# Two of four row tiles turned by DMA instead of PE, and the last weights moved behind those transposes

## The chip, the cores and the metric

The kernel runs on one core of a Trainium2 chip. The metric is device time in microseconds (us); lower is better. All timed runs of this study were in the fast state; the few that ran at a lower mean granted clock (0.991; the granted clock is the share of its full speed at which the matmul engine may run) are named where they matter.

One core has a matmul engine (PE, whose weight loads are listed as PEld), VectorE (DVE), ScalarE (ACT), GpSimd (POOL) and a queue of DMA issues on SyncE (SPq). ACT can issue DMAs too (ACTq). The profile counts the core's DMA work over 16 DMA engines. In its views `arena` is the kernel's one large buffer on the chip and PS are the banks that PE writes. A DMA has *landed* when all its parts have arrived; the *slack* of a transfer is the time from its landing to its first use.

## The reference, cut to what matters

```python
x = A_x                                   # 2048 rows of 512, bf16
xn = layernorm(x)                         # (x - mean) / sqrt(var + eps)
return x + ssm(xn) + (gelu(xn @ w_gate) * (xn @ w_up)) @ w_down   # 1376 hidden columns
# ssm: a complex diagonal recurrence over the rows, between two projections, plus xn * Dskip
```

The rows are worked in four blocks of 512, and a block in four tiles of 128 rows. This kernel's matmuls take a tile with its 512 features on the partitions (the rows of the buffer), so each normalised tile has to be turned.

## The kernel before

A helper records every operation with what it reads and writes; a scheduler orders DVE, ACT and POOL, while PE and the sync queue keep the order of the program. Block 0 is special: PE would otherwise wait for the normalisation, so its four tiles are only centred, turned on PE, and matmuls on the gate and up columns 0 to 895 start at once. The division by sigma is done afterwards, as the `scale` of the gelu and of the product. The rest of the hidden columns (896 to 1375, weight chunk 3) and the Bu projections use the normalised block turned by DMA, with 512 rows per matmul; I call those matmuls *block-wide*.

```python
def cent_T(j, banks, engs="A"):           # turn centred tile j on PE: 4 transposes + copy from PSUM by ACT
    ...
    ins_ = e.transpose(pt[:, 128*q:128*(q+1)], XN[j].ap[:, 128*k:128*(k+1)], IDN.ap)
    ...
FR = ((0, 192), (192, 384), (384, 640), (640, 896))
def unit(j, r):                           # tile j, column range r: gate and up matmuls, gelu, product
    bank = next_bank()
    GT_mm(j, r, bank, [0, 1])             # lhs XCd(j, k): the tile turned on PE
    GT_evac(j, r, bank, rss[j])           # rss[j] = 1/sigma of tile j
# loads on the sync queue, in this order (x tile 1, second half of gate chunk 0 and the
# three parameter rows are on the scalar queue):
#   x0, gate0 (first half), x2, up0, x3, gate1, up1, gate2, up2, gate3, up3,
#   transpose of the parameters, transposes of tiles 0, 1, 2, 3, x of block 1, B ...
fill(2); cent_T(0, tb, "AA"); cent_T(1, [wb])
... # tile 0 and 1, ranges 0 and 1: gate columns, then up columns; cent_T(2) in between
unit(2, 0); unit(2, 1)
cent_T(3, [ub[0, 0]])
unit(0, 2); unit(1, 2); unit(3, 0); unit(3, 1); unit(2, 2); unit(3, 2)
norms(0, [2, 3], mn2, rq2, 2)
TR(0)                                     # all four tiles turned by DMA into XNT[0]
ld_x(1)
for j in range(4): unit(j, 3)
...
GU(0, [7, 8, 9, 10])                      # block-wide, weight chunk 3
BU(0)                                     # block-wide Bu projections
```

Of the kernel before, what the change touches and what calls it, by code (L numbers as in the profile page):

```python
# [77 lines left out]
class Sched:  # L78
# [95 lines left out]
    def _backward(self, span):  # L174
# [11 lines left out]
        while n:  # L186
            best = None
            for e in ENGINES:
                if e in INORDER:
                    if not last[e] or left[last[e][-1].id]:  # L190
                        continue
                    op = last[e][-1]
                else:
                    if not ready[e]:
                        continue
                    op = max(ready[e], key=lambda o: (min(busy[e], late[o.id]), o.finish, o.id))
                end = late[op.id] if op.kind == "dma" else min(busy[e], late[op.id])
                if best is None or end > best[0]:
                    best = (end, op)
            end, op = best  # L200
            e = op.eng
            if e in INORDER:
                last[e].pop()
            else:
                ready[e].remove(op)
            begin[op.id] = end - op.dur
            if op.kind == "dma":
                begin[op.id] = min(begin[op.id], busy[e] - op.issue)
                busy[e] = begin[op.id]
            else:  # L210
                busy[e] = begin[op.id]
            n -= 1
            for d in op.deps:
                late[d.id] = min(late[d.id], begin[op.id] - LAT(d, op))
                left[d.id] -= 1
                if left[d.id] == 0 and d.eng not in INORDER:
                    ready[d.eng].append(d)
        return begin

    def _forward(self, prio):  # L220
# [13 lines left out]
        def rdy_time(op):  # L234
            return max([d.finish + LAT(d, op) for d in op.deps] + [op.nb])
# [55 lines left out]
    def emit(self):  # L291
# [19 lines left out]
        for e in ENGINES:  # L311
            seen = {}
            prog = []
            for op in order[e]:
                need = {}
                for d in op.deps:
                    if d.kind == "eng" and d.eng == e and (e == "tensor" or d is op.behind):
                        continue
# [43 lines left out]
def d_pe(n_list):  # L362
    return sum(n / 2.4 + 2.5 for n in n_list)
# [3 lines left out]
def d_dve_ts4x(n): return 220.0 + 0.26 * n  # L367
# [5 lines left out]
def build(nc, ins, out):  # L373
    with ExitStack() as es:
# [135 lines left out]
        ld_w(WU, WUc, ins["B_w_up"], 0)  # L510
        ld_x0(3)
        for ci in (1, 2):
            ld_w(WG, WGc, ins["B_w_gate"], ci)
            ld_w(WU, WUc, ins["B_w_up"], ci)

        def load_par():
            for q, nm in enumerate(("A_log_dt", "A_Lambda_re", "A_Lambda_im")):
                S.dma(lambda e, q=q, nm=nm: e.dma_start(PROW.ap[4 * q:4 * q + 4, :], ins[nm].rearrange("(s p) -> s p", p=128)),
                      1024, writes=[PROWq[q]], tag="ld_" + nm, queue="scalar", after=[half])

        def tr_par():
            S.dma(lambda e: e.dma_start_transpose(PAR.ap.rearrange("p q t -> p (q t)").unsqueeze(1), PROW16.ap), 4096,
                  reads=PROWq, writes=[PAR], tag="tr_par", issue=900.0)
# [11 lines left out]

        def load_W():
            ld_w(WG, WGc, ins["B_w_gate"], 3)
            ld_w(WU, WUc, ins["B_w_up"], 3)
# [147 lines left out]
        def GT_mm(j, r, bank, us, ks=range(KD)):  # L686
# [8 lines left out]
            def f(e):  # L695
                ins_ = None
                for k in ks:
                    ins_ = e.matmul(dst, XCd(j, k), WGU[:, us[0]:us[-1] + 1, k, f0:f1], start=(k == 0), stop=(k == KD - 1))  # L698
                return ins_
            PE(f, d_pe([w * len(us)] * len(ks)), Wc + XCs[j][ks[0] // 2:ks[-1] // 2 + 1], [BANK[bank]], "GT")  # L700

        def GT_evac(j, r, bank, rs):
            f0, f1 = FR[r]
            w = f1 - f0
            GATE["nh"] = kk = (GATE["nh"] + 1) % 3
            sc, rb = rs
            GATE["last_gelu"] = ACT(lambda e: e.activation(GG[kk].ap[:, 0:w], PS[bank][:, 0:w], ACTF.Gelu_apprx_tanh, scale=sc),  # L707
                                    d_act(w, 1), [BANK[bank], rb], [GG[kk]], "gelu")
            hp = Buf("H0_%d_%d" % (j, r), "sb", H0[j].lo + 2 * f0, H0[j].lo + 2 * f1)
# [9 lines left out]
        def TR(b):  # L719
            tts = list(range(4 * b, 4 * b + 4))  # L720
            for j, tt in enumerate(tts):
# [213 lines left out]
        load_par()  # L935
        load_W()
        tr_par()
# [3 lines left out]
        ch(V(lambda e: e.tensor_scalar(XN[1].ap, X[1].ap, NM1.ap, None, ALU.add), d_dve_ts4x(512), [X[1], NM1], [XN[1]], "sub"))  # L941
        ch(*stats(0, 1))
        op, mn0, qb0, rq0 = root(0, 0, 2)
        ch(op)
        ch(*stats(0, 2)); ch(sub(2))
        ch(recip(qb0, rq0))
# [3 lines left out]
        cent_T(1, [wb])  # L950
        ub = {(j, r): next_bank() for j in range(2) for r in range(2)}
# [5 lines left out]
        for j in range(2):  # L957
            ch(norms(0, [j], mn0, rq0, 0))
        ch(*stats(0, 3)); ch(sub(3))
        op, mn2, qb2, rq2 = root(0, 2, 4)  # L960
        ch(op)
        ch(recip(qb2, rq2))
        rss = [(rq.ap[:, i:i + 1], rq) for rq in (rq0, rq2) for i in range(2)]
# [6 lines left out]
        for j in range(2):  # L970
            for r in range(2):
                GT_mm(j, r, ub[j, r], [1])
                GT_evac(j, r, ub[j, r], rss[j])
                if j == 0 and r == 0:
                    cent_T(2, tb)
        unit(2, 0); unit(2, 1)
        cent_T(3, [ub[0, 0]])
        unit(0, 2)
        unit(1, 2)
        unit(3, 0); unit(3, 1)  # L980
        unit(2, 2); unit(3, 2)
        norms(0, [2, 3], mn2, rq2, 2)
        TR(0)
        ld_x(1)
        for j in range(4):
            unit(j, 3)
# [89 lines left out]
```

## Time and profile before

| what | before | how to read it |
|---|---|---|
| time, median (all runs beside the change) | 178.34 us (177.96 to 178.51, 6 runs) | device time |
| span of the profiled run | 176.6 us | one execution |
| PE busy | 98% of the span | part 1 of the page |
| chain of waits on PE | 1.02 to 174.1 us without a gap over 0.05 us | the view of the chain |
| last up chunk landed | 13.1 us (issued 7.21, 5.9 us to landing) | the view of DMA issues |

The chain of waits, cut to its first 25 us, for the kernel before. Columns: start in us, length in us, engine or cause, output and line, number of instructions. L698 is the matmuls of single tiles, L673 the PE transposes, L823 the block-wide gate and up matmuls, L734 the Bu matmuls.

```profile
...
7.51 0.22 PE PS L673 x4
7.73 2.32 PE PS L698 x20
10.05 0.22 PE PS L673 x4
10.27 8.21 PE PS L698 x40
...
18.53 5.13 PE PS L823 x23
...
24.98 2.16 PE PS L734 x10
```

PE works through. The two lines of L673 at 7.51 and 10.05 are what the change takes away, 0.22 us each.

The waits of PE in the whole run, for the kernel before: the engine and line that waited, for whom, total us, times, longest.

```profile
PE PS L914 <- DVE arena L479: 1.0, 1, 1.0
```

Only the wait for the first operand at the start.

The sync queue's issues, in order of time, for the kernel before (start, length of the issue, line, operation).

```profile
5.94 1.23 SPq L494 DMA_DIRECT2D arena<-in_B_w_gate_dram  x1
7.21 0.69 SPq L494 DMA_DIRECT2D arena<-in_B_w_up_dram  x1
8.03 1.29 SPq L522 DMA_TRANSPOSE arena<-arena  x1
9.37 5.18 SPq L722 DMA_TRANSPOSE arena<-arena  x4
```

Both last weight chunks are issued right behind the others. They land at 11.8 and 13.1 us; the four transposes, issued from 9.4 to 14.5 us, land between 13.8 and 15.8. PE needs the tiles and the gate chunk at about 18.3 us and the up chunk at about 19.2.

### The profile page before, as it was taken

The numbers are of one execution on the slowest core, as the hardware profiler recorded it, in microseconds if no ns is written. First come the engines' busy times: TensorE is split into PE (matmuls) and PEld (weight loads), VectorE is DVE, ScalarE is ACT, GpSimd is POOL, SyncE is SP. The second block draws the span as 40 slices with busy tenths as digits, with TensorE's granted clock in tenths as the row PEclk, the third lists the DMA queues.
The fourth block names the chain that finished last, engine by engine and source line by source line (L and its number), as shares of the span: only waits on it lengthen the run. The fifth ranks groups of instructions, "written<-read, shape, count | busy, mean of one in ns | idle before, by whom it ended". The sixth has DMA issues, their size and how long they took to land.

```text
span 176.6 us, 2492 instructions
## 1 busy us (share of the span) xinstructions
PE 172.3 (98%) x873; PEld 84.5 (48%) x888; DVE 160.7 (91%) x283; ACT 89.5 (51%) x169; POOL 11.4 (6%) x25
## 2 busy tenths in 40 slices
PE   7999999999999999999999999999999999999994
PEld 2954464444544444444644444444454444444453
DVE  6979999998999979799999999899999999999811
ACT  5565678999666997003676692000767780000000
POOL 3212240200000000500000000000000000000000
PEclk9999999999999999999999999999999999999999
DMA  6997999676899000011025000100001000000311
GB/s 173 312 322 181 162 231 127 63 146 121 176 248 303 11 0 0 0 61 59 4 44 105 2 0 0 33 30 30 30 0 30 4 0 0 0 0 30 111 60 43
DMA packets 33396, 14.36 MB, mean 81 GB/s; under 512 B 23688, under 2 KB 33384, under 8 KB 33384
## 3 DMA queue, kind: packets, MB, share of 16 engines
q1 hardware_dynamic: 32944, 13.87, 35.0%
q10 hardware_dynamic: 440, 0.33, 0.6%
q8 instruction: 7, 0.11, 0.3%
q14 instruction: 5, 0.04, 0.1%
HBM read 6.46 MB, written 2.10 MB: 48 GB/s over the span
## 4 chain that ended last, share of the span: by engine, by line
PE 98%; issue 1%; DVE 0%
PE PS L864 37%; PE PS L823 32%; PE PS L734 16%; PE PS L698 7%; PE PS L797 3%; PE PS L914 2%; PE PS L673 1%; PE PS L921 0%; DVE arena L882 0%; DVE arena L479 0%; DVE arena L478 0%
## 5 line engine op out<-in xcount | busy, mean ns | idle before, releaser
L864 PE MATMUL PS<-arena 128*128 128x512 bf16 (+3 forms) x317 | 65.9, 366 | 0.3
L823 PE MATMUL PS<-arena 128*128 128x512 bf16 x258 | 57.5, 379 | 0.3
L864 PEld LDWEIGHTS PS<-arena 128*128 128x128 bf16 (+1 forms) x323 | 30.9, 98 | 35.2
L823 PEld LDWEIGHTS PS<-arena 128*128 128x128 bf16 x264 | 25.8, 98 | 30.4
L838 ACT ACTIVATE arena<-PS 128x512 bf16<-128x512 f32 x33 | 19.8, 601 | 37.5 <-PE PS L823 33.7
L767 DVE TENSOR_TENSOR_SCAN arena<-arena 128x512 bf16<-128x512 f32 x32 | 38.7, 1255 | 0.0
L734 PE MATMUL PS<-arena 128*128 128x512 bf16 x125 | 27.8, 379 | 0.2
L842 ACT ACTIVATE arena<-PS 128x512 bf16<-128x512 f32 x33 | 19.8, 598 | 5.1 <-PE PS L823 4.9
L734 PEld LDWEIGHTS PS<-arena 128*128 128x128 bf16 x128 | 12.5, 98 | 14.9
L856 ACT ACTIVATE PS<-arena 128x512 f32<-128x512 bf16 (+2 forms) x17 | 9.3, 581 | 17.5 <-DVE arena L882 17.1
L738 ACT ACTIVATE arena<-PS 128x512 bf16<-128x512 f32 x32 | 17.3, 602 | 1.3 <-PE PS L734 1.3
L882 DVE TENSOR_TENSOR arena<-PS,arena 128x512 bf16<-128x512 f32 (+2 forms) x17 | 10.8, 654 | 6.7 <-PE PS L864 6.6
L844 DVE TENSOR_TENSOR arena<-arena 128x512 bf16<-128x512 bf16 x33 | 13.2, 416 | 1.1 <-ACT arena L842 1.1
L698 PE MATMUL PS<-arena 128*128 128x192 bf16 (+2 forms) x80 | 13.0, 320 | 0.0
L624 DVE BATCH_NORM_STATS2 arena<-arena 128x6 f32<-128x512 bf16 x16 | 10.3, 686 | 0.6 <-DMA arena<-in_A_x_dram 0.6
L698 PEld LDWEIGHTS PS<-arena 128*128 128x128 bf16 x80 | 7.3, 100 | 4.7 <-issue 0.2
L756 DVE TENSOR_TENSOR arena<-arena 128x4096 bf16<-128x4096 bf16 (+1 forms) x5 | 9.2, 1861 | 0.3 <-ACT arena L620 0.3
L754 DVE TENSOR_TENSOR arena<-arena 128x4096 bf16<-128x4096 bf16 (+1 forms) x5 | 9.2, 1862 | 0.0
L780 DVE TENSOR_TENSOR arena<-arena 128x4096 bf16<-128x4096 bf16 x4 | 9.2, 2288 | 0.0
L779 DVE TENSOR_TENSOR arena<-arena 128x4096 bf16<-128x4096 bf16 x4 | 9.2, 2288 | 0.0
L707 ACT ACTIVATE arena<-PS,arena 128x192 bf16<-128x192 f32 (+1 forms) x16 | 6.6, 449 | 4.9 <-PE PS L698 4.8
L710 DVE SCALAR_TENSOR_TENSOR arena<-PS,arena 128x192 bf16<-128x192 f32 (+1 forms) x16 | 6.6, 445 | 1.4 <-ACT arena L707 1.3
(84 smaller groups left out, 112.2 us busy)
## 6 DMA issues: line engine op xcount, KB each, us to landing
out_dram<-arena SPq DMA_DIRECT2D x15, 128.0 KB, 1.7
arena<-in_A_x_dram SPq DMA_DIRECT2D x3, 512.0 KB, 5.1
arena<-in_B_w_down_dram SPq DMA_DIRECT2D x1, 1280.0 KB, 8.3
arena<-in_B_w_gate_dram SPq DMA_DIRECT2D x2, 256.0 KB, 5.1
arena<-in_B_w_up_dram SPq DMA_DIRECT2D x2, 256.0 KB, 5.4
arena<-in_B_w_gate_dram SPq DMA_DIRECT2D x1, 480.0 KB, 5.8
arena<-in_B_w_up_dram SPq DMA_DIRECT2D x1, 480.0 KB, 5.9
arena<-arena SPq DMA_TRANSPOSE x25, 2.5
```

What stands on the lines that cost most here:

```text
L624: return (V(lambda e: e.bn_stats(ST[tt].ap, X[tt].ap), d_dve_1x(512), [X[tt]], [ST[tt]], "bnst"), V(lambda e: e.bn_aggr(MVt[b][j].ap, ST[t ...
L698: ins_ = e.matmul(dst, XCd(j, k), WGU[:, us[0]:us[-1] + 1, k, f0:f1], start=(k == 0), stop=(k == KD - 1))
L734: ins_ = e.matmul(PS[bank][:, :], BBT[c][dk].ap[:, 128 * s:128 * (s + 1)], XNT[b].ap[:, dk, :], start=(dk == 0), stop=(dk == KD - 1))
L738: GATE["evBu"] = ACT(lambda e, bank=bank, k3=k3, s=s, c=c: e.activation(SSc[k3][s][c].ap, PS[bank][:, :], ACTF.Copy), d_act(512), [BANK[ba ...
L767: V(lambda e, g=g, rb=rb, init=init: e.tensor_tensor_scan(g.ap, rb, g.ap, init, ALU.mult, ALU.add), d_dve_scan(512), [g, PA[RRr]] + ([CARc ...
L823: ins_ = e.matmul(PS[bank][0:m, c0:c1], W.ap[:, dk, 128 * ft:128 * ft + m], XNT[b].ap[:, dk, c0:c1], start=(dk == 0), stop=(dk == KD - 1))
L838: GATE["last_gelu"] = ACT(lambda e, bg=bg, kk=kk, m=m: e.activation(GG[kk].ap[0:m, :], PS[bg][0:m, :], ACTF.Gelu_apprx_tanh), d_act(512), ...
L842: ACT(lambda e, bu=bu, kk=kk, m=m: e.activation(UPB[kk].ap[0:m, :], PS[bu][0:m, :], ACTF.Copy), d_act(512), [BANK[bu]], [UPB[kk]], "evU")
L844: V(lambda e, kk=kk, m=m, ft=ft, k2=k2: e.tensor_tensor(HTt[k2][ft].ap[0:m, :], GG[kk].ap[0:m, :], UPB[kk].ap[0:m, :], ALU.mult), d_dve_tt ...
L856: ACT(lambda e: e.activation(PS[bank][:, c0:c1], X[tt].ap[:, c0:c1], ACTF.Copy), d_act(c1 - c0), [X[tt]], [BANK[bank]], "seed")
L864: ins_ = e.matmul(PS[bank][:, c0:c1], l_[:, 128 * j:128 * (j + 1)], r_[:, c0:c1], start=False, stop=last and n == len(ops) - 1, skip_group ...
L882: V(lambda e: e.tensor_tensor(OUTB[ko].ap[:, c0:c1], PS[bank][:, c0:c1], XD[tt].ap[:, c0:c1], ALU.add), d_dve_1x(c1 - c0), [BANK[bank], XD ...
```

## The change

Its intent: PE is the limit, so take eight PE transposes away from it (tiles 2 and 3). Those tiles are normalised early and turned by DMA, which block 0 needs anyway for the block-wide part. To let these transposes pass, the last weight chunks go behind them on the sync queue, tiles 0 and 1 being turned around the last of the two. PE does all of tiles 0 and 1 first. The parameters are turned on PE, to free the sync queue, and loaded later. (The diff also changes the scheduler: an operation placed behind a DMA now waits for its issue only.)

```diff
-        ld_w(WU, WUc, ins["B_w_up"], 0)
-        ld_x0(3)
-        for ci in (1, 2):
-            ld_w(WG, WGc, ins["B_w_gate"], ci)
+        for ci in range(3):
+            if ci:
+                ld_w(WG, WGc, ins["B_w_gate"], ci)
+            if ci == 1:
+                ld_x0(3)
             ld_w(WU, WUc, ins["B_w_up"], ci)
 ...
+        def tr_par(bank):                # parameters: one 16-column transpose on PE, copy on ACT
 ...
+                    lhs = XCd(j, k) if j < 2 else XNT[0].ap[:, k, 128 * j:128 * (j + 1)]
 ...                                      # and for j >= 2 gelu and product without 1/sigma
-        load_par()
-        load_W()                         # gate chunk 3, up chunk 3
-        tr_par()
+        ch(*stats(0, 2))                 # tile 2's statistics ahead of tile 1's
+        ...
+        ch(recip(qb2, rq2)); ch(norms(0, [2], mn2, rq2, 2))
+        TR(0, [2])
         fill(2)
         cent_T(0, tb, "AA")
         cent_T(1, [wb])
+        load_par()
+        ...
+        TR(0, [0])
+        ch(recip(qb3, rq3)); ch(norms(0, [3], mn3, rq3, 3)); ch(norms(0, [1], mn0, rq0, 0))
+        TR(0, [3])
+        ld_w(WG, WGc, ins["B_w_gate"], 3)
+        TR(0, [1])
+        ld_w(WU, WUc, ins["B_w_up"], 3)
 ...
-        cent_T(2) and cent_T(3), units of the four tiles mixed, TR(0)
+        # tiles 0 and 1: all four ranges; then
+        tr_par(next_bank())
+        for j in (2, 3):
+            for r in range(4):
+                unit(j, r)
```

The last removed line, and the comments, are words of this text; the diff is otherwise cut, not altered.

More of the change, by code (lines that the diff above doesn't have):

```diff
@@ L213, in _backward @@
             for d in op.deps:
-                late[d.id] = min(late[d.id], begin[op.id] - LAT(d, op))
+                late[d.id] = min(late[d.id], begin[op.id] + d.dur - d.issue if d is op.behind and d.kind == "dma" else begin[op.id] - LAT(d, op))
                 left[d.id] -= 1
@@ L234, in rdy_time @@
         def rdy_time(op):
-            return max([d.finish + LAT(d, op) for d in op.deps] + [op.nb])
+            return max([d.start + d.issue if d is op.behind and d.kind == "dma" else d.finish + LAT(d, op) for d in op.deps] + [op.nb])
         while nleft:
@@ L316, in emit @@
                 for d in op.deps:
-                    if d.kind == "eng" and d.eng == e and (e == "tensor" or d is op.behind):
+                    if d.eng == e and (d is op.behind or d.kind == "eng" and e == "tensor"):
                         continue
@@ L509, in build @@
         ld_x0(2)
-        ld_w(WU, WUc, ins["B_w_up"], 0)
-        ld_x0(3)
-        for ci in (1, 2):
-            ld_w(WG, WGc, ins["B_w_gate"], ci)
+        for ci in range(3):
[3 more added lines that the diff above has]
+                ld_x0(3)
             ld_w(WU, WUc, ins["B_w_up"], ci)
         def load_par():
+            first = GATE["evTA"]
             for q, nm in enumerate(("A_log_dt", "A_Lambda_re", "A_Lambda_im")):
-                S.dma(lambda e, q=q, nm=nm: e.dma_start(PROW.ap[4 * q:4 * q + 4, :], ins[nm].rearrange("(s p) -> s p", p=128)),
-                      1024, writes=[PROWq[q]], tag="ld_" + nm, queue="scalar", after=[half])
-        def tr_par():
-            S.dma(lambda e: e.dma_start_transpose(PAR.ap.rearrange("p q t -> p (q t)").unsqueeze(1), PROW16.ap), 4096,
-                  reads=PROWq, writes=[PAR], tag="tr_par", issue=900.0)
+                S.order_behind(S.dma(lambda e, q=q, nm=nm: e.dma_start(PROW.ap[4 * q:4 * q + 4, :], ins[nm].rearrange("(s p) -> s p", p=128)),
+                                            1024, writes=[PROWq[q]], tag="ld_" + nm, queue="scalar"), first)
+        def tr_par(bank):
+            pt = PS[bank].bitcast(BF16)
+            PE(lambda e: e.transpose(pt[:, 0:16], PROW16.ap, IDN.ap[0:16, 0:16]), 30.0, [*PROWq, IDN], [BANK[bank]], "TP")
+            ACT(lambda e: e.activation(PAR.ap.rearrange("p q t -> p (q t)"), pt[:, 0:16], ACTF.Copy), d_act(16), [BANK[bank]], [PAR], "par")
         def late_loads():
@@ L534, in load_T @@
                       1.2 * 512 * 1024, writes=[b_], tag="tr_" + nm, issue=3000.0)
-        def load_W():
-            ld_w(WG, WGc, ins["B_w_gate"], 3)
-            ld_w(WU, WUc, ins["B_w_up"], 3)
         def load_B():
@@ L697, in f @@
                 for k in ks:
-                    ins_ = e.matmul(dst, XCd(j, k), WGU[:, us[0]:us[-1] + 1, k, f0:f1], start=(k == 0), stop=(k == KD - 1))
+                    lhs = XCd(j, k) if j < 2 else XNT[0].ap[:, k, 128 * j:128 * (j + 1)]
+                    ins_ = e.matmul(dst, lhs, WGU[:, us[0]:us[-1] + 1, k, f0:f1], start=(k == 0), stop=(k == KD - 1))
                 return ins_
-            PE(f, d_pe([w * len(us)] * len(ks)), Wc + XCs[j][ks[0] // 2:ks[-1] // 2 + 1], [BANK[bank]], "GT")
+            PE(f, d_pe([w * len(us)] * len(ks)), Wc + (XCs[j][ks[0] // 2:ks[-1] // 2 + 1] if j < 2 else [XTk[0][j]]), [BANK[bank]], "GT")
         def GT_evac(j, r, bank, rs):
@@ L705, in GT_evac @@
             GATE["nh"] = kk = (GATE["nh"] + 1) % 3
+            hp = Buf("H0_%d_%d" % (j, r), "sb", H0[j].lo + 2 * f0, H0[j].lo + 2 * f1)
+            if rs is None:
+                GATE["last_gelu"] = ACT(lambda e: e.activation(GG[kk].ap[:, 0:w], PS[bank][:, 0:w], ACTF.Gelu_apprx_tanh),
+                                        d_act(w), [BANK[bank]], [GG[kk]], "gelu")
+                V(lambda e: e.tensor_tensor(H0[j].ap[:, f0:f1], PS[bank][:, w:2 * w], GG[kk].ap[:, 0:w], ALU.mult),
+                  d_dve_1x(w), [BANK[bank], GG[kk]], [hp], "hmul")
+                return
             sc, rb = rs
@@ L708, in GT_evac @@
                                     d_act(w, 1), [BANK[bank], rb], [GG[kk]], "gelu")
-            hp = Buf("H0_%d_%d" % (j, r), "sb", H0[j].lo + 2 * f0, H0[j].lo + 2 * f1)
             V(lambda e: e.scalar_tensor_tensor(H0[j].ap[:, f0:f1], PS[bank][:, w:2 * w], sc, GG[kk].ap[:, 0:w], ALU.mult, ALU.mult),
@@ L717, in H0_T, with TR @@
                       3.0 * 224 * 1024, reads=[H0[j]], writes=wr, tag="tr_h0", issue=2100.0)
-        def TR(b):
-            tts = list(range(4 * b, 4 * b + 4))
-            for j, tt in enumerate(tts):
+        def TR(b, js=range(4)):
+            for j in js:
+                tt = 4 * b + j
                 S.dma(lambda e, b=b, j=j, tt=tt: e.dma_start_transpose(
@@ L941, in build @@
         ch(V(lambda e: e.tensor_scalar(XN[1].ap, X[1].ap, NM1.ap, None, ALU.add), d_dve_ts4x(512), [X[1], NM1], [XN[1]], "sub"))
+        ch(*stats(0, 2))
+        op, mn2, qb2, rq2 = root(0, 2, 3)
+        ch(op)
         ch(*stats(0, 1))
@@ L944, in build @@
         ch(op)
-        ch(*stats(0, 2)); ch(sub(2))
-        ch(recip(qb0, rq0))
+        ch(recip(qb2, rq2)); ch(norms(0, [2], mn2, rq2, 2))
+        TR(0, [2])
         fill(2)
@@ L950, in build @@
         cent_T(1, [wb])
+        load_par()
+        ch(*stats(0, 3))
+        ch(recip(qb0, rq0))
+        op, mn3, qb3, rq3 = root(0, 3, 4)
+        ch(op); ch(norms(0, [0], mn0, rq0, 0))
+        TR(0, [0])
[4 more added lines that the diff above has]
+        ld_w(WU, WUc, ins["B_w_up"], 3)
         ub = {(j, r): next_bank() for j in range(2) for r in range(2)}
@@ L956, in build @@
         fill(4)
-        for j in range(2):
-            ch(norms(0, [j], mn0, rq0, 0))
-        ch(*stats(0, 3)); ch(sub(3))
-        op, mn2, qb2, rq2 = root(0, 2, 4)
-        ch(op)
-        ch(recip(qb2, rq2))
-        rss = [(rq.ap[:, i:i + 1], rq) for rq in (rq0, rq2) for i in range(2)]
+        rss = [(rq0.ap[:, i:i + 1], rq0) for i in range(2)] + [None, None]
         def unit(j, r):
@@ L973, in build @@
                 GT_evac(j, r, ub[j, r], rss[j])
-                if j == 0 and r == 0:
-                    cent_T(2, tb)
-        unit(2, 0); unit(2, 1)
-        cent_T(3, [ub[0, 0]])
-        unit(0, 2)
-        unit(1, 2)
-        unit(3, 0); unit(3, 1)
-        unit(2, 2); unit(3, 2)
-        norms(0, [2, 3], mn2, rq2, 2)
-        TR(0)
+        for r in (2, 3):
+            bs = [next_bank(), next_bank()]
+            for j in range(2):
+                GT_mm(j, r, bs[j], [0])
+            for j in range(2):
+                GT_mm(j, r, bs[j], [1])
+                GT_evac(j, r, bs[j], rss[j])
+        tr_par(next_bank())
+        for j in (2, 3):
+            for r in range(4):
+                unit(j, r)
         ld_x(1)
-        for j in range(4):
-            unit(j, 3)
         params()
```

## The prediction

> **What bounds it.** PE. PE is busy for 98% of the 176.6 us span (page), and the chain of waits runs on PE from 1.02 to 174.1 us, with no PE wait longer than about 0.05 us. Mean matmul time (379 ns) is not the cost of one: the Trainium skill ("Trainium Kernel Development and Optimization", Performance Expectations) says matmul busy time misleads because matmuls are pipelined, and this trace agrees: 49 of the 128x512 ones take 10.74 us of the chain, 219 ns each. So time is won only by taking PE work away or shortening the start, and lost by making PE wait.
>
> **Removed.** Two groups of four PE transposes for tiles 2 and 3: the chain shows 0.22 us at 7.51 and 0.22 us at 10.05, 0.44 us in all. Off the critical path: two ACT copies (0.6 us each), two centrings on DVE (0.36 each), one DMA transpose of the parameters (1.29 us of the sync queue).
> **Added.** One 16-column PE transpose, estimated 0.05 us from the 0.055 of one transpose, a small ACT copy, two more tiny DVE/POOL operations. The up/gate work on PE stays. Net on PE: -0.39 us.
> **Moved.** PE does all of tiles 0 and 1 first, then tiles 2 and 3 from the DMA transposes. The start is unchanged.
>
> **New waits, from landings in the trace before (issue plus time to landing) against estimated need on PE** (chain rates: 192-column matmul 82 ns, 256-column 107 ns):
> - up chunk 0 lands 6.8, needed 7.2. Gate chunk 1: about 7.6 against 8.5. Up 1: 8.8 against 9.3. Gate 2: 9.6 against 10.2. Up 2: 10.5 against 11.1. Half a microsecond of slack.
> - Tile 2: x lands 5.5, so its statistics now make DVE wait and push tile 1's by about 1.1 us; normalised about 8.4, transposed (2.6 us when the queue is free) about 11.2, needed 11.9.
> - Tile 3: normalised 11.5, landed 14.3, needed 14.9.
> - First gelu waits for 1/sigma of tiles 0, 1: about 9.5 instead of 7.6. Eight PSUM banks cover it: first reuse by PE (parameters) near 11.9, that bank free about 10.5.
> - Last gate chunk issued about 12.9, lands 17, needed 18.1. Last up chunk waits in the queue behind tile 1's transpose, which waits for DVE (about 13.2): issued about 14.8, lands about 18.5, needed 18.9. This is the tightest; a stall of 0 to 0.6 us is possible.
> - Loads of block 1 and the B transposes start about 0.8 us later (15.2 to 16); B_re lands about 23.3 to 24, needed 24.4.
>
> **Predicted.** -0.39 us plus an expected stall of about 0.15 us: 178.47 - 0.25 = 178.2 us; range 177.5 to 179.0. Faster by over 2%: 0.01; within 2%: 0.97; slower: 0.02. The runs before spread more (177.96 to 178.51).
>
> **What would show it.** Right: the first block-wide matmuls (L823 before, at 18.53) start near 18.1; the chain stays 98% PE; no PE wait above 0.1 us; first gelu near 9.5; the order of transposes 2, 0, 3, 1 at about 8.4, 10.1, 11.5, 13.5. Wrong: PE idle "DMA" before tile 2's or tile 3's matmuls, before the first block-wide up matmuls (last up weights), or before the first Bu matmuls (B_re).
>
> **What would make it wrong.** A DMA transpose queued behind 2 MB of weights landing later than I assume (each late microsecond goes straight to the time); the sync queue blocked by a transpose whose DVE input is late, so that weights and B come late; a PE stall long enough to lower the clock granted (0.999 now); evacuations on DVE falling behind, so that PE waits for banks in tile 3.

## The result, and the profile after

The changed kernel took 179.12 us (median of 6 runs, 178.71 to 179.26) against 178.34 for the kernel before. The ratio is 1.0042 with a 95% interval of 1.0027 to 1.0057. (A ratio is the mean time of one kernel's fast runs over the mean of the other's in the same rounds, so it is not quite the ratio of the medians quoted.) That is within 2%, but it is a loss clear of noise, and outside the predicted range of 177.5 to 179.0.

The chain of waits of the changed kernel, its first 25 us. L698 is the tile matmuls, L525 the parameters' transpose, L829 the block-wide gate and up matmuls, L740 Bu.

```profile
1.43 4.65 DMA arena<-in_B_w_gate_dram
...
6.13 0.51 PE PS L698 x4
...
6.86 5.47 PE PS L698 x56
12.33 0.11 PE PS L525
12.44 6.17 PE PS L698 x32
18.61 0.14 issue
18.75 0.43 DVE arena L710
19.18 1.02 PE PS L829 x4
...
20.25 4.49 PE PS L829 x20
...
26.06 4.10 PE PS L740 x19
```

The transposes are gone, yet Bu starts at 26.06 instead of 24.98. Three gaps explain it: PE waited before 6.13 for half of a gate chunk, from 18.61 to 19.18 before the first block-wide matmul, and around 20.2 before the up matmuls. The chain measures the last two badly: it counts a 512-column matmul as busy for 0.38 us, while the next one starts 0.22 us after it, and in the kernel before one of the 24 block-wide matmuls is missing from the record (x23). So I take them from the starts of the matmuls in the trace. The last tile matmul started at 18.22, so the first block-wide one was due at 18.43; it started at 19.18, 0.75 us late. The fifth, the first that reads the last up chunk, was then due at 20.04 and started at 20.25, another 0.21 us. (The 0.57 and 0.42 us in the expectations below are the chain's figures for the two.)

PE's waits in the changed kernel:

```profile
...
PE PS L829 <- DVE arena L710: 0.6, 1, 0.6
PE PS L698 <- DMA arena<-in_B_w_gate_dram: 0.4, 1, 0.4
```

The work that the change takes from PE also shows in the starts. The timeline of PE, for the kernel before and for order_b (a variant below with the changed kernel's work on PE, and no wait in this stretch), from the four fillers of the start (matmuls on dummy data) to the block-wide matmuls:

```profile
6.13 0.39 PE L921 MATMUL PS<-arena 128*128 128x128 bf16 x4
...
18.53 5.13 PE L823 MATMUL PS<-arena 128*128 128x512 bf16 x23
```

```profile
5.93 0.39 PE L927 MATMUL PS<-arena 128*128 128x128 bf16 x4
...
18.12 5.13 PE L829 MATMUL PS<-arena 128*128 128x512 bf16 x23
```

That is 12.40 us before and 12.19 with the change: 0.2 us less, where 0.44 went away with the transposes. The parameters' transpose costs most of the rest. The chain gives it 0.11 us, but it also starts 0.20 us after a matmul whose successor otherwise comes after 0.11, in every profile of the changed order: about 0.2 us together.

The sum for the changed kernel is -0.22 (work, its own starts) + 0.34 (its fillers started at 6.47 instead of 6.13) + 0.75 + 0.21 = +1.08 us, against the 1.09 us by which Bu started later. The two waits near 19 us are not two causes that add up. Had tile 1 been in time, the up matmuls would have been due at 19.30, and the late up chunk would have held them until 20.25 all the same: it alone sets the 0.95 us.

From there on nothing differs: from the first Bu matmul to the end of PE's work it is 149.28 us in both kernels, read from the starts of the matmuls in the traces, and 149.28 to 149.31 in every kernel profiled below. So the whole story lies in the first 25 us.

The sync queue of the changed kernel:

```profile
8.59 3.97 SPq L728 DMA_TRANSPOSE arena<-arena  x3
12.60 0.58 SPq L494 DMA_DIRECT2D arena<-in_B_w_gate_dram  x1
13.23 1.19 SPq L728 DMA_TRANSPOSE arena<-arena  x1
14.47 0.58 SPq L494 DMA_DIRECT2D arena<-in_B_w_up_dram  x1
```

Its DMA issues in windows around the issues at 8.59, 12.60, 13.23 and 14.47 (size, then us from issue to landing):

```profile
arena<-arena SPq DMA_TRANSPOSE x1, 2.7
...
arena<-in_B_w_gate_dram SPq DMA_DIRECT2D x1, 480.0 KB, 4.4
...
arena<-arena SPq DMA_TRANSPOSE x1, 5.8
...
arena<-in_B_w_up_dram SPq DMA_DIRECT2D x1, 480.0 KB, 5.7
```

Tile 2's transpose, issued 2.3 us before the last load ahead of it landed (10.9), took 2.7 us. Tile 1's, issued behind the gate chunk, took 5.8 and landed at 19.0; PE started at 19.18. The up chunk landed at 20.2; its matmuls started at 20.25. PE could have used them at 18.4 and 19.3. In both, a few of the 16 parts came last: 15 parts of tile 1 were there by 17.5, and half of the up chunk's by 18.9.

The profile puts the wait at 18.6 down to DVE L710, a product of tile 3. That cannot be what PE waited for: the bank that the first block-wide matmul writes had been emptied by 14.2, when tile 2's first product (L710) ended. It was a matter for experiment.

### The profile page after: what moved, and what is told of

It reads as the page before. It is cut to its first block, busy times and chain, and to the rows that moved or that the text cites. A ratio compares the mean times of both kernels' runs of the same rounds, so it can differ in the third digit from the quotient of the medians.

```text
span 177.5 us, 2529 instructions
## 1 busy us (share of the span) xinstructions
PE 173.1 (98%) x897; PEld 85.3 (48%) x897; DVE 160.0 (90%) x283; ACT 87.7 (49%) x168; POOL 11.2 (6%) x27
## 4 chain that ended last, share of the span: by engine, by line
PE 95%; DMA 3%; DVE 0%; ACT 0%; issue 0%
PE PS L870 37%; PE PS L829 32%; PE PS L740 16%; PE PS L698 7%; PE PS L803 3%; DMA arena<-in_B_w_gate_dram 3%; ACT L480 0%; DVE arena L710 0%; DVE arena L888 0%; PE PS L927 0%; PE PS L525 0%
## 5 line engine op out<-in xcount | busy, mean ns | idle before, releaser
L829 PE MATMUL PS<-arena 128*128 128x512 bf16 x264 | 58.3, 379 | 0.6 <-DVE arena L710 0.6
L829 PEld LDWEIGHTS PS<-arena 128*128 128x128 bf16 x264 | 25.7, 98 | 31.5 <-issue 1.0
L740 PE MATMUL PS<-arena 128*128 128x512 bf16 x128 | 28.1, 379 | 0.0
L740 PEld LDWEIGHTS PS<-arena 128*128 128x128 bf16 x128 | 12.5, 98 | 14.9
L888 DVE TENSOR_TENSOR arena<-PS,arena 128x512 bf16<-128x512 f32 (+2 forms) x17 | 10.9, 654 | 8.3 <-PE PS L870 7.9
L862 ACT ACTIVATE PS<-arena 128x512 f32<-128x512 bf16 (+2 forms) x17 | 9.3, 581 | 17.6 <-DVE arena L888 17.1
L698 PE MATMUL PS<-arena 128*128 128x192 bf16 (+3 forms) x96 | 12.9, 291 | 0.4 <-DMA arena<-in_B_w_gate_dram 0.4
L698 PEld LDWEIGHTS PS<-arena 128*128 128x128 bf16 x96 | 8.7, 98 | 3.9 <-DMA arena<-in_B_w_gate_dram 0.6
L642 DVE TENSOR_SCALAR arena<-arena 128x512 bf16<-128x512 bf16 x16 | 6.1, 408 | 0.1
L803 PE MATMUL PS<-arena 128*128 128x192 bf16 x64 | 5.9, 246 | 0.0
```

The costliest lines, as they stand in the source:

```text
L698: ins_ = e.matmul(dst, lhs, WGU[:, us[0]:us[-1] + 1, k, f0:f1], start=(k == 0), stop=(k == KD - 1))
L740: ins_ = e.matmul(PS[bank][:, :], BBT[c][dk].ap[:, 128 * s:128 * (s + 1)], XNT[b].ap[:, dk, :], start=(dk == 0), stop=(dk == KD - 1))
L803: ins_ = e.matmul(dst, XNT[b].ap[:, dk, 128 * j:128 * (j + 1)], WGU[:, :, dk, f0:f0 + m], start=(dk == 0), stop=(dk == KD - 1))
L829: ins_ = e.matmul(PS[bank][0:m, c0:c1], W.ap[:, dk, 128 * ft:128 * ft + m], XNT[b].ap[:, dk, c0:c1], start=(dk == 0), stop=(dk == KD - 1))
L888: V(lambda e: e.tensor_tensor(OUTB[ko].ap[:, c0:c1], PS[bank][:, c0:c1], XD[tt].ap[:, c0:c1], ALU.add), d_dve_1x(c1 - c0), [BANK[bank], XD ...
```

## The experiments

All ran with five rounds beside the kernel before. None reached 2%: by that measure each kernel here is the same as the kernel before, and scalar_queue_old unclear; what follows is about differences below it. A first look at PE's waits gave theory A: the loss is the late queue order of the last weights and of tile 1. Its rivals were B (PE waits for DVE and banks, as the profile names it), C (noise of one profile) and, for the start, D (chance) against F (the changed load order). Two came later: E (one DMA engine late with tile 1) and G (what counts is lateness against a slack of under 0.6 us).

### The changed kernel again

No edit.

> The changed kernel unchanged, for a second profile. In the first one PE waited 0.40 us for the second half of gate chunk 0 (the load on the scalar queue, landed 6.1 us), 0.57 us before the first block-wide matmul (19.18) and about 0.42 us before the first block-wide up matmuls (last up chunk, landed 20.2). Theory A (the late queue order of the last weights and of tile 1's transpose is the loss): the last two waits return within 0.3 us each. Whether the 0.40 us wait returns is open: if it is chance of the start, it will be gone here and the time is about 178.7; if it belongs to the change it returns and the time is 179.1. Rival C (noise of one profile): none of the three returns.

It took 179.12 us (178.44 to 179.67), ratio 1.0037 (1.0017 to 1.0057). The wait at 6 us was gone, the wait for tile 1 was gone, and the wait for the last up chunk was larger. PE's waits:

```profile
...
PE PS L829 <- DMA arena<-in_B_w_up_dram: 0.7, 1, 0.7
```

So rival C falls for the up chunk, which came late both times (here it was issued at 15.09 and landed at 19.8; by the starts PE waited 0.83 us). The other two waits vary from run to run: tile 1, behind the same gate chunk, took 4.0 us this time and landed at 17.0, in time. The up chunk was issued 0.6 us later than in the first profile, because the issue of tile 1's transpose ahead of it lasted 2.02 us instead of 1.19, about until tile 3's transpose had landed (15.1). The expectation that 178.7 follows if the 0.40 us is chance was wrong, since the late up chunk alone cost nearly as much (0.83 us) as both late arrivals had (0.95).

### Tile 1 turned before the last weights

```diff
+        TR(0, [1])
         ld_w(WG, WGc, ins["B_w_gate"], 3)
-        TR(0, [1])
         ld_w(WU, WUc, ins["B_w_up"], 3)
```

The order on PE, DVE, ACT and POOL is the same as in the changed kernel; only the sync queue differs.

> Only the sync queue differs from the changed kernel: tile 1's transpose is issued before both last weight chunks (2, 0, 3, 1, gate, up); the order on PE, DVE, ACT and POOL is the same. Theory A (the wait at 18.6 to 19.2 is for tile 1's transpose, stuck behind the last gate chunk in the queue): tile 1 lands near 15.4, gate chunk near 18.2 to 18.4, up chunk near 19.5; the 0.57 us wait shrinks to under 0.1, the up wait stays at 0 to 0.4 us; time about 0.5 us below the changed kernel, 178.6. Rival B (PE waits for DVE to empty a bank, as the profile names it): DVE is untouched, so the wait stays at 0.57 us and the time at 179.1.

178.97 us (178.48 to 179.72), ratio 1.0032. Tile 1, issued near 12.7, took 2.4 us to land, and the wait at the first block-wide matmul shrank from 0.75 to about 0.1 us by the starts (0.57 to 0.15 in the view), now behind the gate chunk, which landed at 18.4. As DVE was untouched, this speaks against rival B, though weakly, since the second profile of the changed kernel lacked that wait without any edit; stronger is that the bank was free. The time fell by 0.15 us only, not 0.5, which does not stand clear of noise. Its chain shows why: the up chunk, needed near 19.3, came late as before.

```profile
14.60 5.07 DMA arena<-in_B_w_up_dram
...
19.71 4.49 PE PS L829 x20
```

Besides, PE had waited 0.4 us for up chunk 0 near 7 us in this profile. Taking away one late arrival left the one that set the time.

### Queue in the order of need

```diff
+        ld_w(WG, WGc, ins["B_w_gate"], 3)
         TR(0, [3])
+        ld_w(WU, WUc, ins["B_w_up"], 3)
+        TR(0, [0])
         TR(0, [1])
```

Tile 2 stays first. The scheduler reorders some DVE and ACT work with this, so it is not as clean as the last one.

> Sync queue reordered by need: tile 2, last gate chunk, tile 3, last up chunk, tile 0, tile 1. Theory A: the gate chunk is issued near 9.9 and lands near 14, tile 3 near 14.5 (needed 15.5), the up chunk near 16.5 (needed 19.3), tile 1 near 17.5 to 18 (needed 18.6): no PE wait at the block-wide matmuls; about 1.0 us below the changed kernel, 178.1, so 0.2 to 0.4 below the kernel before if the 0.40 us wait at the start stays away. Rival B (DVE, banks): no gain, 179.1. What could spoil it: tile 3's transpose late behind the gate chunk, seen as a PE wait near 15.5.

178.45 us, ratio 1.0006 (0.9977 to 1.0035), with times in two groups: 177.81, 177.99, 178.02 and 178.87, 179.28, 179.32. The profile was of the fastest run. Its timeline of PE (start, busy, line, count):

```profile
11.88 6.23 PE L698 MATMUL PS<-arena 128*128 128x384 bf16 x32
18.16 5.13 PE L829 MATMUL PS<-arena 128*128 128x512 bf16 x23
```

No wait at the block-wide matmuls, and Bu started at 24.45 by the timeline, against 24.81 in the kernel before: 0.36 us earlier. That this is near the prediction's net of 0.39 is luck: the four fillers at the start had come 0.37 us earlier (5.76 instead of 6.13), and of the 0.2 us of saved work a pause of 0.17 us before 12 us took most. In order_b, where nothing came late, the fillers were 0.20 us and Bu 0.40 us earlier, so the saved work of 0.2 us is real when nothing comes late. (One block-wide matmul is missing from both records, so the starts of L829 are read 0.22 us late.)

### The same once more

> The interleaved queue order once more, because its six times fell in two groups (177.8 to 178.0, and 178.9 to 179.3). Theory D (chance in the landings of the first 2 MB of loads, which the new order of PE meets with about half a microsecond of slack): both groups come again, and if the profiled run is of the slower group its profile shows PE waits of about 1 us in sum between 5 and 12 us or before tile 2. Theory E (one of the 16 DMA engines late with the transpose of tile 1, as in the changed kernel's first profile): the slower group's profile shows the wait at 18.0 before the first block-wide matmul instead.

178.93 us (178.27 to 179.16), ratio 1.0027. This time the profiled run took 179.14. PE's waits:

```profile
PE PS L829 <- DVE arena L610: 1.0, 1, 1.0
...
PE PS L698 <- DMA arena<-in_B_w_gate_dram: 0.4, 1, 0.4
...
```

Chance at the start (D) and a late tile 1 (E, one DMA engine late) both appear in one run: 0.4 us at 6 us and 1.0 us at 18.3. The larger one was tile 1 again, landed at 19.1 (issued at 14.3, 4.7 us); tile 0's transpose ahead of it had landed only at 18.6. This is where the DMA view tells something new. First, the queues in the window 15.2 to 16.6 us, then in the window 16.55 to 17.45 us (packets, MB, share of the 16 engines' time):

```profile
q1 hardware_dynamic: 813, 0.42, 219.7%
q8 instruction: 1, 0.02, 5.6%
...
q1 hardware_dynamic: 64, 0.02, 84.1%
```

In the first window an instruction fetch of 16 KB (the instruction queue, q8) occupied 5.6% of 16 engines for 1.4 us, which is 1.25 us of a single engine. In the second window the engines counted as 84% busy and moved only 0.02 MB in 0.9 us, where the rate of the first window (0.42 MB in 1.4 us) would have given 0.27. In the trace, most packets that stand open there are those of transposes (they end together near 17.85), and the only packets of a load that still complete are a dozen of the up chunk, at 6 to 7% of the engines' time, about one engine. My reading is that one engine, held by the fetch, made the transposes wait for it. In the run of the first group the fetch fell at 20.9 us, after everything was in. In the two profiles of the changed kernel it fell at 16.95 (when tile 1's transpose landed late: one of 16 parts came 1.5 us after the others) and at 13.0 us. There tile 1 was in time, but tile 3's transpose, in flight at 13.0, took 4.0 us instead of 2.5, and behind it the issue of tile 1 and of the up chunk slipped. Against it stands old_start: its fetch, from 17.1 to 18.4, overlapped tile 1's transpose, which landed at 17.9 without a visible delay. Over all profiles the fetch falls anywhere from 13 to 21 us. I could not move it on purpose, so its part is observed, not tested.

### Tile 0 in the gap

```diff
         ld_w(WG, WGc, ins["B_w_gate"], 3)
+        TR(0, [0])
         TR(0, [3])
         ld_w(WU, WUc, ins["B_w_up"], 3)
-        TR(0, [0])
         TR(0, [1])
```

> Tile 0's transpose fills the gap before tile 3's is ready: tile 2, gate, tile 0, tile 3, up, tile 1. Tile 1's transpose is then issued near 12.7 instead of 14.0 and lands near 16.8 instead of 17.0 to 17.5 (needed 18.0). Theory E: the slower group of times thins out, median about 178.0. Theory D: the spread stays, median about 178.3.

178.76 us (177.78 to 180.30), ratio 1.0028 (0.9993 to 1.0062). The profiled run was the fastest one, 177.78, and had no wait at 18 us. The slower times did not thin out, so an earlier tile 1 alone does not cure it. Only the profiled run can be looked into; what delayed the 180.30 stays unknown.

### The start of the loads as before

order_b, with x tile 3 ahead of gate chunk 1 and the parameter rows loaded early:

```diff
-        for ci in range(3): ... ld_x0(3) behind gate chunk 1 ...
+        ld_w(WU, WUc, ins["B_w_up"], 0)
+        ld_x0(3)
+        for ci in (1, 2): ...
-        cent_T(1, [wb]); load_par()
+        load_par()                       # at the start, as in the kernel before
```

> As order_b, but the start of the loads is as in the kernel before: x tile 3 ahead of gate chunk 1, the three parameter rows loaded on the scalar queue right after gate chunk 0. Theory D as chance: early landings scatter as in the others (up chunk 0 at 6.7 to 7.3), time as order_b within 0.2 us. Theory F (the new start itself slows the first loads): up chunk 0 lands near 6.8 in the profile, no PE wait before 7 us, and the time is 0.3 us or more below order_b with a spread like that of the kernel before (0.7 us).

178.48 us (178.03 to 179.17), ratio 1.0011 (0.9986 to 1.0036), which lies between the two theories by time. Its profile speaks against F: up chunk 0 landed at 7.6 us, later than in any other profile, although its loads were in the old order, and PE paused before 7.6 us. Over all profiles the four fillers behind gate chunk 0 start at 6.04 to 6.52 us with the old start (six profiles) and at 5.76 to 6.47 with the new one (eight), so the start scatters by half a microsecond in both kernels. Landings are one reason. The other is PE's clock, which I had overlooked: at first its matmuls come at half the pace (192 columns 0.16 us apart, later 0.08), and the trace's first record of the full granted clock begins anywhere from 3.97 us (interleaved_2) to 7.00 us (tile3_only_2), at 5.74 in the kernel before and 5.30 in the changed one. The 0.40 us wait for the second half of gate chunk 0 came in two of the eight profiles with the new start and in none of the six with the old one. It may be chance, but that is too few to exclude F for it.

### The kernel before with those transposes doubled

```diff
-                    for q in range(per):
+                    for q in [*range(per)] * (2 if j >= 2 else 1):
```

> The kernel before with the eight PE transposes of tiles 2 and 3 issued twice (same result). The price put on them is 0.44 us for eight, so the time rises by 0.44 us (178.4 to 178.9) and the first block-wide matmuls come 0.44 us later. If PE has hidden slack there, it rises by less. Its loads are untouched, so its profile is a second look at the start of the kernel before: up chunk 0 near 6.8 if the kernel before has steadier landings, up to 7.3 if they scatter there too.

178.92 us (178.75 to 179.18), ratio 1.0034 (1.0018 to 1.0051), which is 0.61 us with an interval of 0.32 to 0.91. In the timeline of PE, a doubled group and the matmuls after it:

```profile
7.82 0.61 PE L673 MATMUL PS<-arena 128*128 128x128 bf16 x8
8.26 2.45 PE L698 MATMUL PS<-arena 128*128 128x192 bf16 x20
```

From 7.82 to 8.26 is 0.44 us for eight transposes, 0.055 each. The price was right, and PE has no slack there that would hide it. In this profile the first block-wide matmul came 0.89 us later than in the kernel before, not 0.44: the rest was lost before the first doubled group, which started 0.48 us late, the full clock having come at 6.76 us.

### Both last chunks ahead of the transposes

```diff
+        ld_w(WG, WGc, ins["B_w_gate"], 3)
+        ld_w(WU, WUc, ins["B_w_up"], 3)
         TR(0, [2])
```

(and removed below).

> Both last weight chunks are loaded ahead of all four transposes, in the kernel-before's order. Theory A predicts that the two waits at the block-wide matmuls go, but that tile 2's transpose, issued near 8.6, lands near 13.9 behind 960 KB of weights, as tile 0's did in the kernel before (13.8), so PE waits about 1.5 us at 12.4 before tile 2's matmuls: time about 179.6, 0.5 above the changed kernel. If transposes are not held by loads ahead of them in the queue, tile 2 lands at 11.3 and the time is about 178.1.

179.96 us (179.57 to 180.31), ratio 1.0087. PE's waits:

```profile
PE PS L698 <- DMA arena<-arena: 1.4, 1, 1.4
...
```

As theory A says: the waits at 18 us are gone, and tile 2's transpose, issued at 8.2 behind 960 KB, lands at 13.7. This is what the change avoided by moving the weights. Each order makes something late.

### The last chunks on the scalar queue

```diff
-        ch(recip(qb2, rq2)); ch(norms(0, [2], mn2, rq2, 2))
+        ch(recip(qb2, rq2)); n2 = norms(0, [2], mn2, rq2, 2); ch(n2)
+        ld_w(WG, WGc, ins["B_w_gate"], 3, "scalar", [n2])
+        ld_w(WU, WUc, ins["B_w_up"], 3, "scalar", [n2])
         TR(0, [2])
```

Tile 1 is normalised right behind tile 0. The second kernel has the old start of the loads as well.

> The last gate and up chunks go on the scalar engine's DMA queue, right after tile 2 is normalised (about 8.4), so they no longer stand before or behind the transposes in one queue; tile 1 is normalised right after tile 0; the sync queue has the transposes 2, 0, 3, 1. Theory G (the loss is lateness of the last weights and of tile 1 against a slack of under 0.6 us, made worse by the 16 KB instruction fetch that holds one DMA engine for about 1.2 us somewhere between 13 and 21 us): both chunks land by about 14.5, tile 1 by about 16, over 2 us before they are needed, so no PE wait at the block-wide matmuls in any run: median 178.0 to 178.1, spread about as in the kernel before. If the weights now slow tile 2's transpose, PE waits near 12 instead.

> The same with the start of the loads as in the kernel before (x tile 3 ahead of gate chunk 1, parameter rows early). Theory D (the first landings scatter by chance): same time as scalar_queue within 0.2 us. Theory F (the new start slows the first loads): 0.3 us or more below scalar_queue.

Both lost: 179.98 us (179.94 to 181.73, one run of six at a mean clock of 0.991), ratio 1.0117, and 182.01 us, ratio 1.0186 (1.0153 to 1.0219). The main expectation (178.0 to 178.1) failed, and its escape clause came true. Issues of scalar_queue near 8 us:

```profile
arena<-in_B_w_gate_dram ACTq DMA_DIRECT2D x1, 480.0 KB, 4.2
arena<-in_B_w_up_dram ACTq DMA_DIRECT2D x1, 480.0 KB, 5.7
arena<-arena SPq DMA_TRANSPOSE x1, 5.8
```

A second queue did not let the transpose pass: it took 5.8 us beside the loads, much as it did behind them (5.5 in weights_first), and PE waited 1.5 us for tile 2. The Trainium skill ("DMA: Bandwidth & Descriptors", Issuing engines are not separate DMA queues) says that DMAs from all engines run on the same 16 DMA engines and interleave; this run agrees.

The second kernel paid twice. Its PE by window, start and end in us, length, busy and count, granted clock, DMA share, GB/s:

```profile
14.90:16.50 1.60, 1.59 (x9) 0.85 1.24 274
16.50:19.40 2.90, 2.90 (x8) 0.50 1.18 296
19.40:22.40 3.00, 3.00 (x17) 0.99 0.89 215
```

After a wait of 2.8 us (12.1 to 14.9) PE ran at half clock; the second window lies within that stretch, which lasts 3.4 us in the trace, from 16.0 to 19.4; five of its six timed runs had a mean clock of 0.991. The Trainium skill ("TensorE: Matmul & The Clock Gate", Part 1) puts the drop at one idle window of about 3.4 us; here 2.8 us of waiting was enough. (The clock's records in this trace change at 5.78, 16.02 and 19.43 us, about three and one times 3.41 us apart. If the page's window runs on in such steps, an inference, the one before the drop began at 12.61 us, and PE was idle for 2.3 us of it.) As the clock differs between these two kernels, they don't test D against F.

### Half of the change, on the kernel before

Tile 2 stays on PE. Only tile 3 is turned by DMA, and it is used last; the weights keep their unbroken stream.

```diff
-        ch(*stats(0, 3)); ch(sub(3))
+        ch(*stats(0, 3))
 ...
-        ch(recip(qb2, rq2))
+        ch(recip(qb2, rq2)); ch(norms(0, [3], mn2, rq2, 2))
+        TR(0, [0, 3, 1])
 ...
         unit(2, 0); unit(2, 1)
-        cent_T(3, [ub[0, 0]])
-        ... units of tiles 0 to 3 mixed, norms(0, [2, 3]), TR(0)
+        for r in (2, 3):
+            for j in range(3): unit(j, r)
+        norms(0, [2], mn2, rq2, 2)
+        TR(0, [2])
+        ld_x(1)
+        for r in range(4): unit(3, r)     # from XNT[0], without 1/sigma
```

> Half of the change, on the kernel before: tile 2 stays turned on PE, only tile 3 is normalised early and turned by DMA, and its matmuls come last; the weights keep their unbroken stream and the parameters their DMA transpose. PE loses four transposes, 0.22 us by the price of 0.055 us each. Theory G (slack decides): tile 3 lands near 14, behind the last weights (13.1), and is needed near 15.2; tiles 0 to 2 and both last chunks land 3 us or more before the block-wide matmuls at 18.1. So no new PE wait, and the whole 0.22 us shows: ratio to the kernel before 0.9988, first block-wide Bu matmul 0.22 us earlier in the profile, and a spread like that of the kernel before (0.8 us), not the 1.2 to 2.5 of the others. Rival (any transpose by DMA costs PE more than it saves): ratio 1.003 or above, with a PE wait near 15.

> The same kernel again, because its first interval (0.9978 to 1.0006) does not separate a gain of 0.22 us (0.9988) from none. In its first profile PE lost about 0.36 us to late first loads (before 7.3 us), which the kernel before also risks, and had no wait at the DMA-turned tile. Theory G: ratio 0.9988 again, no PE wait after 8 us; the Bu matmuls start at 24.5 if the first loads are early, 24.8 if not. If the two ratios differ by more than 0.002 in opposite directions, the gain is not shown.

178.26 us (178.15 to 178.33, 5 runs), ratio 0.9992 (0.9978 to 1.0006); then 178.16 us (177.85 to 178.56, 6 runs), ratio 0.9986 (0.9970 to 1.0002). Both sit around the expected 0.9988, and neither interval excludes 1, so a gain over the kernel before is likely but not shown. Against the changed kernel it is clearly better. The chain of the first of these runs:

```profile
2.17 5.01 DMA arena<-in_B_w_up_dram
...
7.73 0.22 PE PS L673 x4
7.95 10.52 PE PS L699 x60
18.47 5.18 PE PS L831 x24
```

After the first loads (up chunk 0 at 7.18 us, 0.4 us later than in the profile of before) PE works through: one group of PE transposes is left, and the DMA-turned tile, landed near 14.6, costs no wait. In this profile the late load ate the gain, so Bu did not start 0.22 us earlier as I had expected; it started at the same time. In the second profile (178.56 us, the slowest of its six) Bu started at 25.22 us by the timeline, 0.41 later than in the kernel before and outside the expected 24.5 to 24.8, though PE had no wait after 8 us; there the full clock had come only at 7.00 us. From the fillers to the block-wide matmuls this variant saves 0.2 us as well (without its wait of 0.3 us for up chunk 0). Half of the change thus frees as much of PE as all of it, since it leaves the parameters' transpose to the DMA.

## Why the prediction was wrong

- **What bounds it, and the price of the removed work: right.** PE was the limit. Eight transposes at 0.44 us were confirmed by the doubled run (a group doubled to eight took 0.44 us).
- **The price of the added work: wrong, by nearly half of the forecast gain.** The parameters' transpose was put at 0.05 us and cost about 0.2, so the net on PE was about -0.2 us, not -0.39.
- **"Eight PSUM banks cover it": right.** No run showed a wait for a bank, though the profile named DVE at the wait.
- **The first 12 us: right about order, too confident about slack.** "Half a microsecond of slack" is the size of the scatter of the first landings (up chunk 0 from 6.6 to 7.6 us), and the moment at which PE's full clock comes scatters too. Both hit the kernel before as well.
- **Tiles 2 and 3: right.** They landed in time (at 11.3 and 13.8 us; predicted 11.2 and 14.3), with no wait.
- **The step that failed is "This is the tightest; a stall of 0 to 0.6 us is possible", counted as 0.15 us.** By the starts of the matmuls the stall was 0.95 us in the first profile and 0.83 in the second. Over the runs, the loss of 0.75 us (0.42% of 178.3) plus the net gain of 0.2 us makes a mean stall of about 1.0 us, an estimate, with what the start may have lost in it. The sign that the prediction had named for being wrong, PE idle before the first block-wide up matmuls, is the one that came. The size that was wrong is the landing of the last up chunk. It was taken to land 3.7 us after its issue (14.8 to 18.5, needed 18.9); it took 5.7 and 4.8 us in the two profiles, landed at 20.2 and 19.8, and was needed at 19.3 and 19.1. Tile 1, to which the prediction gave no landing time, took 5.8 and 4.0 us behind the gate chunk, and 2.4 with that chunk moved behind it; it was late only in the first profile, within the up chunk's own delay. Why the up chunk takes so long is not isolated. Two things are seen: its last parts come alone (from 18.7 to 20.2 us, half of them by 18.9), and a load that follows a pause or a transpose starts slowly. A window from 12.5 to 15.0 us of the changed kernel, with the gate chunk issued at 12.60 and 40 rates of 0.06 us each:

```profile
GB/s 25 119 197 233 225 221 217 221 209 209 147 58 17 0 0 0 0 0 0 0 0 31 77 108 108 31 92 92 61 0 31 61 108 123 31 15 15 46 61 108
```

  The first quarter is a transpose ending. The gate chunk's first bytes come near 13.85 us, and the rate stays at or under 123 GB/s until 15.0, 2.4 us after its issue. From 16.9 to 17.9 us, when the up chunk followed tile 1's transpose, it was 214 GB/s on average. In the kernel before, the same chunk was part of a stream that ran at 336 GB/s on average from 5.9 to 11.0 us.
- **The form of the error.** I treated each landing as one number and kept the stall at what the sum left over. With several arrivals, each with a slack of about half a microsecond and a scatter as large, the expected wait is that of the latest. The kernel before had four to six microseconds of slack for tile 1 and the last weights. The Trainium skill ("DMA: Bandwidth & Descriptors", Rules for kernel authors) advises issuing a DMA early and waiting for it late; the change did the reverse for 960 KB to save 0.2 us of PE time.
- **What stays open:** how much of the scatter comes from the instruction fetch. It was seen to coincide with late transposes in three profiles, overlapped one without delay, and was not tested; how much of the spread of the times is the moment of PE's full clock, which no run held fixed; why the last up chunk's parts straggle; and order_b's 180.30, which has no profile.

## What to carry to other kernels

When the limiting engine has no gaps, freeing it of small work pays only if no transfer it depends on loses its slack: list for each moved transfer landing time and need, and ask for a slack of more than the scatter seen between runs, here about a microsecond. Price small added work on the limiting engine as well: one 16-column transpose cost here about as much as four of the 128-column ones. Keep a stream of loads unbroken, because a late restart costs more than the bytes (the gate chunk took 4.4 us; its 480 KB at the stream's 336 GB/s would be 1.5 us, an estimate); and look at what stands ahead of a DMA in its queue, not only at its own duration. If the whole change fails, try the half of it that leaves the critical transfers alone: turning only the last-used tile by DMA kept the loads as they were and did not lose.

## What the Trainium skill lacked or had wrong

- No page has it that an instruction fetch can hold up a DMA transpose; it would belong to "Runtime: NRT & Kernel Launch". In one run a 16 KB fetch took 1.25 us of one DMA engine, and right after it the engines counted as 84% busy for 0.9 us while moving 0.02 MB. Observed, not tested.
- "DMA: Bandwidth & Descriptors", Rules for kernel authors, says, where it warns of corrupted results, that a transpose next to ordinary DMAs "needs nothing". That held (all outputs were correct). What it lacks is the cost in time: a transpose took 4.0 to 5.8 us behind or beside 480 KB loads, and 2.4 to 2.5 us with no load ahead of it.
- "Advanced Engine Details and Errata", X-Bar Transpose, gives transposes the speed of regular DMAs; it lacks this dependence (2.4 to 5.8 us, above) on what shares the engines.
- "DMA: Bandwidth & Descriptors", Latency and other measured facts, gives about 0.6 us to the first byte. Here the first packet of a load that followed a transpose came 1.25 us after the start of its issue, which itself lasted 0.58 us, so about 0.67 us after its end; the page doesn't say from where it counts. What it lacks is the slow rise: full rate came about 2.4 us after the start of the issue.
- "TensorE: Matmul & The Clock Gate", Part 1, ties the drop to half clock to an idle window of about 3.4 us. A wait of 2.8 us was followed, 1.1 us after PE had started again, by 3.4 us at a granted clock of 0.50.
